# First batch of a fused attention and feed-forward kernel in units of 128, 256 and 384 tokens, with keys ahead of queries and weights in column quarters

## Chip, cores, metric

One NeuronCore of one Trainium2 chip. The metric is the device time of one execution in microseconds (us). TensorE is PE in the profile, VectorE is DVE, ScalarE is ACT, GpSimd is POOL, SyncE is SP.

## The reference

Routed attention (4 batches, 8 heads, 768 tokens of 64), then a SwiGLU feed-forward block with RMS norm (3072 x 512, inner size 1536):

```python
q_assign = argmax(q_n . c_n); k_assign = argmax(k_n . c_n)      # 16 clusters per head
scores = where(q_assign == k_assign, scale * q @ k.T, -1e9)     # per batch and head
attn = softmax(scores) @ v                                       # [4, 8, 768, 64]
x = attn.transpose(0, 2, 1, 3).reshape(3072, 512)
xn = x / sqrt(mean(x * x, -1) + 1e-6) * rms_g
out = (silu(xn @ w_gate) * (xn @ w_val)) @ w_out                 # [3072, 512], fp32
```

## The kernel before

It works in *units* of 384 tokens, two per batch. A unit is attention over 8 heads (three steps of two 384-column score matmuls and one exponential of 768 columns each), then the feed-forward part. Attention waits on ACT, so the feed-forward work of the unit before is given out between the score steps as filler. The order is fixed by the program, and each engine takes its instructions in that order. The accumulators of a head pair have **one** PSUM buffer, which DVE must empty before the next pair can start:

```python
ps_s = pool("ps_s", 2, space=PSUM); ps_a = pool("ps_a", 1, space=PSUM); ps_g = pool("ps_g", 3, space=PSUM)

def pv(u, h):                              # attention times values of one head
    if h % 2 == 0:
        accs[u] = ps_a.tile([P, 2, HT, D + 1], F32, tag="acc", name="acc")
    ...                                    # 18 matmuls into acc
    if h % 2:
        nc.vector.reciprocal(inv, acc[:, :, :, D])
        nc.vector.tensor_tensor(dst, acc[:, :, :, :D], ...)     # the eviction, into x
```

DVE makes the keys of a coming group of four heads (`kcast`: eight casts). For group 2 they are part of `second`, the preparation that fills unit 1 and precedes the transposes of the normed tokens:

```python
def second(h=h, n=n):                      # in group_work(g)
    trans(g, h, 1)
    qcast(g, h)
    kcast(g, h)                            # DVE
    vcast(n); load_qk(n + NQ); load_v(n + NV)

# the list that fills unit 1
prep = group_work(2) + group_work(3)
fill += [rms(0)] + prep[:8] + ffn[:12] + [output_weights] + spread(ffn[12:], prep[8:])   # shortened; ffn = xtrans x4, gv x16
```

In unit 0, which has no feed-forward work to fill it, ten filler matmuls (`busy(1, False)`) are emitted between the score steps.

The softmax here doesn't subtract the row's maximum and nothing guards it: scores larger than these inputs give would overflow.

Of the kernel before, what the change touches and what calls it, by code (L numbers as in the profile page):

```python
# [22 lines left out]
def kernel(  # L23
# [23 lines left out]
    NU = 2 * B  # L47
# [4 lines left out]
    WARM = 5  # L52
# [25 lines left out]
    def load_qk(n, kq=None):  # L78
        if n >= B * H:
            return  # L80
        staged[n] = stage.tile([P, 2, ST, D], F32, tag="qk", name="qk")
        nc.sync.dma_start(out=staged[n][:, 0], in_=src(q, n))
        (kq or nc.sync).dma_start(out=staged[n][:, 1], in_=src(k, n))
# [9 lines left out]
    for n in range(HG):  # L93
        load_qk(n, nc.scalar)
    for n in range(HG, NQ):
        load_qk(n)
# [17 lines left out]
    def rsqrt(ms, n):  # L114
        half = small.tile([P, n], I32, tag=f"half{n}", name="half")
        nc.vector.tensor_scalar(half, ms.bitcast(I32), 1, None, op0=ALU.logical_shift_right)
        yi = small.tile([P, n], I32, tag=f"yi{n}", name="yi")
        nc.vector.tensor_scalar(yi, half, -1.0, float(0x5F3759DF), op0=ALU.mult, op1=ALU.add)
        y = yi.bitcast(F32)
        for i in range(3):  # L120
            a = small.tile([P, n], F32, tag=f"na{n}", name="na")
            nc.vector.scalar_tensor_tensor(a, y, -0.5, y, op0=ALU.mult, op1=ALU.mult)
            a2 = small.tile([P, n], F32, tag=f"nb{n}", name="nb")
            nc.vector.tensor_mul(a2, a, ms)
            y2 = small.tile([P, n], F32, tag=f"ny{n}", name="ny")
            nc.vector.scalar_tensor_tensor(y2, a2, 1.5, y, op0=ALU.add, op1=ALU.mult)
            y = y2
        return y
# [51 lines left out]
    def load_gv(c):  # L180
        nc.gpsimd.dma_start(out=wg[:, c], in_=moe_w_gate[c * P:(c + 1) * P])
        nc.gpsimd.dma_start(out=wv[:, c], in_=moe_w_val[c * P:(c + 1) * P])
# [7 lines left out]
    def trans(g, h, part):  # L190
        if (h % 2, part) == (0, 0):
            qkT[g, h // 2] = qk32.tile([P, 2, 2, UQ], F32, tag="qkT", name="qkT")
# [7 lines left out]
    def qcast(g, h):  # L200
        for e in range(2):
            nc.gpsimd.tensor_copy(qext[g % 4][:D, h, e * UQ:(e + 1) * UQ], qkT[g, h // 2][e * D:(e + 1) * D, h % 2, 0])  # L202

    def kcast(g, h, early=False):
        for e in range(2):
            to, of = kext[g % 4][:D, h, e * UQ:(e + 1) * UQ], qkT[g, h // 2][e * D:(e + 1) * D, h % 2, 1]
            if early:
                nc.scalar.activation(to, of, ACT.Copy, scale=1.0 / ZS)
            else:
                nc.vector.tensor_scalar_mul(to, of, 1.0 / ZS)  # L210
# [11 lines left out]
    def cluster_steps(g, m, h0=0, h1=HG, early=False):  # L222
# [17 lines left out]
        def back():  # L240
            oh = asg.tile([P, UQ], BF16, tag="oh", name="oh", bufs=4)
            nc.vector.transpose(oh[r], of["ohT"][r])  # L242
            put.append((g, (kext if m else qext)[g % 4], oh, h0, h1))
# [13 lines left out]
    put = []  # L257

    def place(qq, kq):

        (g, *_, h0, h1) = put[0]
        for h in range(h0, h1):
            for (_, ext, oh, _, _), on in zip(put, (qq, kq)):
                for e in range(2):
                    on.dma_start(out=ext[D:D + NC, h, e * UQ:(e + 1) * UQ],  # L265
                                 in_=oh[32 * h + e * NC:32 * h + (e + 1) * NC])
        put.clear()
# [4 lines left out]
    def scores(u, h, i):  # L272
        b, hf = divmod(u, 2)
        g, hh = b * 2 + h // HG, h % HG
        if i == 0:
            pT[u, h] = ptp.tile([P, ST, UQ], BF16, tag="pT", name="pT")
        ps = ps_s.tile([P, 2, 512], F32, tag="s", name="s")
        for j in range(2):
            kc = 2 * i + j
            nc.tensor.matmul(ps[:, j, :UQ], lhsT=kext[g % 4][:KR, hh, kc * P:(kc + 1) * P],  # L280
                             rhs=qext[g % 4][:KR, hh, hf * UQ:(hf + 1) * UQ], start=True, stop=True)
        nc.scalar.activation(pT[u, h][:, 2 * i:2 * i + 2], ps[:, :, :UQ], ACT.Exp, bias=off, scale=scale * ZS)  # L282
# [3 lines left out]
    def pv(u, h):  # L286
        b = u // 2
# [6 lines left out]
        for t in range(HT):  # L294
# [3 lines left out]
        if h % 2:  # L298
            inv = small.tile([P, 2, HT], F32, tag="inv", name="inv")
            invs[u] = inv  # L300
            nc.vector.reciprocal(inv, acc[:, :, :, D])  # L301
            dst = xs[u][:, :, (h - 1) * D:(h + 1) * D].rearrange("p t (h d) -> p h t d", d=D)
            nc.vector.tensor_tensor(dst, acc[:, :, :, :D], inv.unsqueeze(3).broadcast_to([P, 2, HT, D]), op=ALU.mult)
# [13 lines left out]
    def rms(u):  # L317
        x = xs[u]
        for t in range(HT):
            squares(u, t, True)  # L320
        ss = small.tile([P, HT], F32, tag="sm", name="sm")
        nc.vector.tensor_add(ss, sq[u][:, 0], sq[u][:, 1])
        ms = small.tile([P, HT], F32, tag="ms", name="ms")
        nc.vector.tensor_scalar(ms, ss, 1.0 / DM, 1e-6, op0=ALU.mult, op1=ALU.add)
        y = rsqrt(ms, HT)
        for t in range(HT):
# [4 lines left out]
    def xtrans(u, c):  # L331
# [3 lines left out]
        for t in range(HT):  # L335
            nc.tensor.transpose(ps[:, t * P:(t + 1) * P], xn[u][:, t, c * P:(c + 1) * P], ident)
        nc.vector.tensor_scalar_mul(xnT[u][:, c], ps, gcol[:, c:c + 1])
# [3 lines left out]
    def gv(u, f, val):  # L341
# [3 lines left out]
        ps = ps_g.tile([P, UQ], F32, tag="gen", name="val" if val else "gate")  # L345
        for c in range(CC):
            nc.tensor.matmul(ps, lhsT=w[:, c, f * P:(f + 1) * P], rhs=xnT[u][:, c], start=c == 0, stop=c == CC - 1)  # L347
        last = u == NU - 1
        if not val:
            th = gate.tile([P, UQ], F32, tag="th", name="th")  # L350
            if last:
                nc.scalar.activation(th, ps, ACT.Silu)
                gates[u] = th
            else:
                nc.scalar.activation(th, ps, ACT.Tanh, scale=0.5)  # L355
                nc.vector.scalar_tensor_tensor(th, th, 1.0, ps, op0=ALU.add, op1=ALU.mult)  # L356
                gates[u] = th
        elif last:
            nc.vector.tensor_mul(gvT[u][:, f], gates[u], ps)
        else:  # L360
            nc.vector.scalar_tensor_tensor(gvT[u][:, f], gates[u], 0.5, ps, op0=ALU.mult, op1=ALU.mult)  # L361
# [3 lines left out]
    def out_mm(u, t, part):  # L365
        b, hf = divmod(u, 2)
# [4 lines left out]
        if part == 2:  # L371
# [3 lines left out]
            nc.sync.dma_start(out=rows[:, 2 * t + hf], in_=o)  # L375


    def group_work(g):
# [15 lines left out]
        w.append((0.0, lambda: place(nc.gpsimd, nc.gpsimd)))  # L394
# [14 lines left out]
    def ffn_work(u):  # L409
        w = [(0.18, lambda c=c: xtrans(u, c)) for c in range(CC)]  # L410
        for f in range(FC):
            w.append((0.64, lambda f=f: gv(u, f, False)))
            w.append((0.64, lambda f=f: gv(u, f, True)))
        return w

    def out_work(u):
        return [(0.86, lambda t=t, p=p: out_mm(u, t, p)) for t in range(HT) for p in range(3)]


    def t0(h):  # L420
        for part in range(2):
            trans(0, h, part)
        qcast(0, h)
        if NQ + h < H:
            load_qk(NQ + h)
# [3 lines left out]

    trans(0, 0, 0)  # L430
    centroids_t()
    trans(0, 0, 1)
    load_qk(NQ)
    trans(0, 1, 0)
    qcast(0, 0)
    qcast(0, 1)
    clusters0(0, 0)
    trans(0, 1, 1)
    load_qk(NQ + 1)
    for n in range(HG):  # L440
        load_v(n)
    clusters0(0, 1)
    for h in range(2, HG):
        for part in range(2):
            trans(0, h, part)
        qcast(0, h)
    place(nc.gpsimd, nc.sync)
    for n in range(HG, H):
        load_v(n)
    nc.sync.dma_start(out=gcol, in_=moe_rms_g.rearrange("(c p) -> p c", p=P), allow_slow_non_contiguous=True)  # L450
    kcast(0, 0, True)
    kcast(0, 1, True)
    vcast(0)
    vcast(1)
    for m in range(2):
        clusters0(2, m)
    for h in range(HG):
        for part in range(2):
            trans(1, h, part)
        qcast(1, h)  # L460
        if h == 1:
            place(nc.gpsimd, nc.sync)
            vcast(2)
            vcast(3)
    busy(2)

    def second_group():
        kcast(0, 2, True)
        kcast(0, 3, True)
        for m in range(2):  # L470
            scores_c(1, m)
        for c in range(CC):
            load_gv(c)
        for n in range(HG, H):
            vcast(n)
        place(nc.sync, nc.sync)
        for h in range(HG):
            kcast(1, h)

    def output_weights():  # L480
# [86 lines left out]
```

## Time and profile before

| | before |
|---|---|
| time | 375.94 us, median of 3 (375.48 to 376.34) |
| span of the profiled run, mean granted clock | 371.8 us, 0.982 |
| output weights, issue to landing (median) | 13.5 us |
| key and query cluster rows ("placements", 12 KB), 10 to 32 us | 2.3 to 5.2 us median by queue |

The prediction below shows the busy shares, the clock and the stretches of this profile.

(Timeline: start, length, engine, line, operation, count, idle time before it. Names: `s` scores, `pT` exponentials, `acc` attention times values, `x` a unit's attention output, `xn` the normed tokens, `tx` and `xnT` the same transposed, `tq` transposed queries or keys, `qext` and `kext` queries and keys with their cluster rows, `th` a gate after tanh, `gvT` gate times val, `o` outputs, `wo` the output weights.) I call what lies between them **the stage**: attention of the last 384 tokens of the first batch, 42.8 us long here. The changed kernel has exactly the same stage as its unit 2.

### The profile page before, as it was taken

The numbers are of one execution on the slowest core, as the hardware profiler recorded it, in microseconds if no ns is written. First come the engines' busy times: TensorE is split into PE (matmuls) and PEld (weight loads), VectorE is DVE, ScalarE is ACT, GpSimd is POOL, SyncE is SP. The second block draws the span as 40 slices with busy tenths as digits, with TensorE's granted clock in tenths as the row PEclk, the third lists the DMA queues.
The fourth block names the chain that finished last, engine by engine and source line by source line (L and its number), as shares of the span: only waits on it lengthen the run. The fifth ranks groups of instructions, "written<-read, shape, count | busy, mean of one in ns | idle before, by whom it ended". The sixth has DMA issues, their size and how long they took to land.

```text
span 371.8 us, 8016 instructions
## 1 busy us (share of the span) xinstructions
PE 351.1 (94%) x3026; PEld 210.5 (57%) x3026; DVE 241.7 (65%) x573; ACT 260.0 (70%) x461; POOL 107.6 (29%) x221
## 2 busy tenths in 40 slices
PE   7979867999999999999999999999999999999995
PEld 3535544565566555655566555655566656664552
DVE  4981186678756966777756966777656565667432
ACT  4797983798669775888668775888767876762320
POOL 3694071089615170325315170325300000000000
PEclk9976998999999999999999999999999999999999
DMA  8649999726126101450022001000020002001002
GB/s 273 188 95 210 249 329 248 159 63 180 58 85 198 63 20 56 129 155 14 13 85 86 4 20 57 30 0 13 12 86 2 3 0 86 2 1 58 28 3 85
DMA packets 24967, 32.03 MB, mean 86 GB/s; under 512 B 4960, under 2 KB 20832, under 8 KB 24928
## 3 DMA queue, kind: packets, MB, share of 16 engines
q1 hardware_dynamic: 18288, 24.72, 20.5%
q0 software_dynamic: 6064, 6.00, 8.6%
q10 hardware_dynamic: 576, 0.79, 0.6%
q8 instruction: 24, 0.39, 0.4%
q14 instruction: 15, 0.12, 0.1%
HBM read 28.35 MB, written 6.29 MB: 93 GB/s over the span
## 4 chain that ended last, share of the span: by engine, by line
PE 71%; ACT 12%; DVE 11%; issue 3%; DMA 1%; DVEq 0%; SPq 0%; ACTq 0%
PE o L370 17%; PE gate L347 13%; PE val L347 13%; PE s L280 13%; PE acc L296 7%; ACT pT L282 7%; PE tq L196 3%; PE sc L251 3%; DVE th L356 2%; ACT th L355 2%; DVE kext L210 2%; ACT qkT L198 1%; ACT xn L315 1%; DVE oh L242 1%; DVE o_sb L373 1%
## 5 line engine op out<-in xcount | busy, mean ns | idle before, releaser
L282 ACT ACTIVATE pT<-s,off 128x768 bf16<-128x768 f32 x192 | 170.9, 902 | 48.3 <-PE s L280 47.3
L280 PE MATMUL s<-qext,kext 80*128 80x384 bf16 x384 | 96.6, 335 | 5.6 <-ACT pT L282 5.2
L347 PE MATMUL val<-xnT,wv 128*128 128x384 bf16 x384 | 78.7, 327 | 0.9 <-DVE th L356 0.6
L347 PE MATMUL gate<-xnT,wg 128*128 128x384 bf16 x384 | 78.9, 327 | 0.1
L370 PE MATMUL o<-wo,gvT 128*128 128x512 bf16 x288 | 70.3, 379 | 0.5
L356 DVE SCALAR_TENSOR_TENSOR th<-th,gate 128x384 f32<-128x384 f32 x84 | 46.4, 553 | 30.3 <-ACT th L355 29.2
L280 PEld LDWEIGHTS <-kext 80*128 80x128 bf16 x384 | 37.2, 100 | 45.2 <-issue 18.5
L202 POOL CAST qext<-qkT 64x384 bf16<-64x384 f32 x64 | 33.7, 526 | 97.2 <-ACT qkT L198 95.3
L355 ACT ACTIVATE th<-gate 128x384 f32<-128x384 f32 x84 | 41.2, 490 | 25.9 <-PE gate L347 22.0
L361 DVE SCALAR_TENSOR_TENSOR gvT<-th,val 128x384 bf16<-128x384 f32 x84 | 46.3, 552 | 9.1 <-PE val L347 2.6
L296 PEld LDWEIGHTS <-pT 128*128 128x128 bf16 x1152 | 44.9, 99 | 9.7 <-issue 0.8
L347 PEld LDWEIGHTS <-wv 128*128 128x128 bf16 x384 | 36.5, 98 | 23.7 <-issue 3.2
L347 PEld LDWEIGHTS <-wg 128*128 128x128 bf16 x384 | 36.6, 98 | 22.7 <-issue 0.7
L296 PE MATMUL acc<-vbf,pT 128*128 128x65 bf16 x1152 | 47.0, 195 | 0.5 <-ACT pT L282 0.5
L370 PEld LDWEIGHTS <-gvT 128*128 128x128 bf16 x288 | 26.7, 97 | 26.2 <-issue 1.0
L265 POOL DMA_DIRECT2D qext<-oh x56 | 27.2, 491 | 39.5 <-DVE oh L242 38.5
L196 PE MATMUL tq<-ident_f,qk 128*128 128x128 f32 x192 | 32.6, 289 | 3.1 <-DMA qk<-in_q_dram 1.2
L198 ACT COPY qkT<-tq 128x384 f32<-128x384 f32 x64 | 29.1, 484 | 5.8 <-PE tq L196 5.6
L210 DVE TENSOR_SCALAR kext<-qkT 64x384 bf16<-64x384 f32 x56 | 24.6, 440 | 12.0 <-ACT qkT L198 11.2
L196 PEld LDWEIGHTS tq<-ident_f,qk 128*128 128x128 f32 x192 | 22.8, 145 | 12.8 <-ACT qkT L198 3.2
L265 POOL DMA_DIRECT2D kext<-oh x48 | 23.3, 489 | 16.6 <-DVE inv L301 15.0
L373 DVE COPY o_sb<-o 128x512 f32<-128x512 f32 x24 | 16.4, 689 | 12.9 <-PE o L370 12.7
(60 smaller groups left out, 232.0 us busy)
## 6 DMA issues: line engine op xcount, KB each, us to landing
qk<-in_q_dram SPq DMA_DIRECT2D x32, 192.0 KB, 3.9
vs<-in_v_dram SPq DMA_DIRECT2D x32, 192.0 KB, 3.8
out_dram<-o_sb SPq DMA_DIRECT2D x24, 256.0 KB, 2.0
qk<-in_k_dram SPq DMA_DIRECT2D x28, 192.0 KB, 3.8
wg<-in_moe_w_gate_dram POOLq DMA_DIRECT2D x4, 384.0 KB, 9.1
wv<-in_moe_w_val_dram POOLq DMA_DIRECT2D x4, 384.0 KB, 10.3
wo<-in_moe_w_out_dram POOLq DMA_DIRECT2D x3, 512.0 KB, 13.5
qext<-oh POOLq DMA_DIRECT2D x56, 12.0 KB, 1.6
```

The source lines that it names most:

```text
L196: nc.tensor.transpose(ps[:, i * P:(i + 1) * P], qk[:, part, 2 * i:2 * i + 2].rearrange("p t d -> p (t d)"), ident_f)
L198: nc.scalar.copy(qkT[g, h // 2][:, h % 2, part], ps)
L202: nc.gpsimd.tensor_copy(qext[g % 4][:D, h, e * UQ:(e + 1) * UQ], qkT[g, h // 2][e * D:(e + 1) * D, h % 2, 0])
L265: on.dma_start(out=ext[D:D + NC, h, e * UQ:(e + 1) * UQ], in_=oh[32 * h + e * NC:32 * h + (e + 1) * NC])
L280: nc.tensor.matmul(ps[:, j, :UQ], lhsT=kext[g % 4][:KR, hh, kc * P:(kc + 1) * P], rhs=qext[g % 4][:KR, hh, hf * UQ:(hf + 1) * UQ], start=T ...
L282: nc.scalar.activation(pT[u, h][:, 2 * i:2 * i + 2], ps[:, :, :UQ], ACT.Exp, bias=off, scale=scale * ZS)
L296: nc.tensor.matmul(acc[:, h % 2, t], lhsT=pT[u, h][:, kc, t * P:(t + 1) * P], rhs=vbf[g % 4][:, hh, kc % HT * 2 + kc // HT], start=kc == 0 ...
L347: nc.tensor.matmul(ps, lhsT=w[:, c, f * P:(f + 1) * P], rhs=xnT[u][:, c], start=c == 0, stop=c == CC - 1)
L355: nc.scalar.activation(th, ps, ACT.Tanh, scale=0.5)
L356: nc.vector.scalar_tensor_tensor(th, th, 1.0, ps, op0=ALU.add, op1=ALU.mult)
L361: nc.vector.scalar_tensor_tensor(gvT[u][:, f], gates[u], 0.5, ps, op0=ALU.mult, op1=ALU.mult)
L370: nc.tensor.matmul(outs[u], lhsT=gvT[u][:, f, t * P:(t + 1) * P], rhs=wo[:, f], start=f == 0, stop=f == FC - 1)
```

## The change

Intent: reach feed-forward work earlier. The first 128 tokens are a unit of their own, so their norm can run after 18 instead of all 24 of the first exponentials; the next 256 are interleaved with them by heads; keys are prepared and placed ahead of queries, so that the first scores start earlier; gate and value weights arrive in column quarters, so that the first quarter suffices for the first gates. The diff, cut to its core:

```diff
-    NU = 2 * B
+    UNITS = [(0, 0, 1), (0, 1, 2), (0, 3, 3)] + [(b, c, HT) for b in range(1, B) for c in (0, HT)]   # batch, first tile, tiles
+    NU = len(UNITS)
-    WARM = 5
+    WARM = 8
-    def load_gv(c):
-        nc.gpsimd.dma_start(out=wg[:, c], in_=moe_w_gate[c * P:(c + 1) * P])
-        nc.gpsimd.dma_start(out=wv[:, c], in_=moe_w_val[c * P:(c + 1) * P])
+    def load_gv(i):
+        c = slice(i * DF // 4, (i + 1) * DF // 4)
+        for w, of in ((wg, moe_w_gate), (wv, moe_w_val)):
+            nc.gpsimd.dma_start(out=w[:, :, c], in_=of[:, c].rearrange("(c p) f -> p c f", p=P))
@@ start: heads 2 and 3 of group 0 get their keys from GpSimd, half of the query columns is placed first
+    for h in (2, 3):
+        kcast(0, h, nc.gpsimd)
+    vcast(2)
+    vcast(3)
+    load_gv(0)
+    def second_clusters():
+        scores_c(1, 0)
+        place(nc.gpsimd, 1, 0, 0, (0,))
+        for h in range(HG):
+            kcast(1, h)
+        ...                                  # value casts, three weight quarters, other query halves, output weights
@@ the order of units
-    for u in range(NU): ...                  # one unit after the other; filler matmuls in unit 0
+    f0 = ffn_work(0)
+    attention([(0, 0), (0, 1), (1, 0), (1, 1), (0, 2), (0, 3), (1, 2), (1, 3), (0, 4), (0, 5), (0, 6), (0, 7)], [],
+              hooks={(0, 1, 0): second_q, (1, 0, 1): second_clusters, (0, 7, 0): second_batch})
+    attention([(1, h) for h in range(4, H)], f0[:CC + 8], 5, {(1, 4, 1): lambda: rms(0)})
+    for u in range(2, NU):
+        ...                                  # as before, with the leftovers, norm and outputs of units of any size
```

The output weights are now issued in the first attention stretch, before any gate, and no filler matmul is left in it.

## The prediction

> **What bounds the kernel now.** I read the page's busy shares and slices first, then the busy time by stretch, then the timelines of PE, ACT, DVE and GpSimd up to 100 us, and last the DMA issues.
>
> ```profile
> PE 351.1 (94%) x3026; PEld 210.5 (57%) x3026; DVE 241.7 (65%) x573; ACT 260.0 (70%) x461; POOL 107.6 (29%) x221
> ...
> PEclk9976998999999999999999999999999999999999
> DMA  8649999726126101450022001000020002001002
> ```
>
> TensorE is the bound over the whole, so any time at which it does no useful work at the start is paid in full at the end. The clock and DMA rows show that only the first sixth is different: the clock dips there, and the DMA engines are full there and nowhere else.
>
> ```profile
> 20.00:30.00 10.00, 7.10 (x61) 3.98 (x54) 8.53 (x18) 8.62 (x13) 9.78 (x20) 0.70 0.50 92
> 30.00:40.00 10.00, 9.73 (x100) 5.69 (x99) 0.77 (x3) 8.52 (x11) 1.85 (x4) 0.79 1.10 215
> 40.00:50.00 10.00, 7.29 (x72) 4.66 (x71) 3.42 (x13) 9.92 (x25) 1.68 (x4) 1.00 0.97 269
> 50.00:60.00 10.00, 5.14 (x49) 3.26 (x48) 8.70 (x20) 4.29 (x9) 7.05 (x12) 0.91 1.04 314
> 60.00:70.00 10.00, 10.00 (x90) 5.75 (x88) 5.61 (x11) 7.87 (x12) 0.00 (x0) 0.92 1.15 251
> ...
> 100.00:200.00 100.00, 99.03 (x915) 61.76 (x914) 70.42 (x166) 74.89 (x130) 30.96 (x64) 1.00 0.27 84
> ```
>
> (Columns: PE, PEld, DVE, ACT, POOL busy; granted clock; DMA share; GB/s.) From 100 us PE is busy 99% at full clock. Before 60 us it is not, and part of its busy time is filler (17 `warm` matmuls, 7.2 us). ACT is the pacemaker there: 8.5 to 9.9 of 10.
>
> ```profile
> 18.30 0.81 PE L280 MATMUL s<-qext,kext 80*128 80x384 bf16 x4
> 33.92 8.31 ACT L282 ACTIVATE pT<-s,off 128x768 bf16<-128x768 f32 x10 [0.23 <-PE s L280]
> 53.47 4.10 DVE L210 TENSOR_SCALAR kext<-qkT 64x384 bf16<-64x384 f32 x8
> 58.08 0.44 PE L336 MATMUL tx<-ident,xn 128*128 128x128 bf16 x3 [3.58 <-DVE xnT L337]
> 58.40 1.44 PE L347 MATMUL gate<-xnT,wg 128*128 128x384 bf16 x4
> 62.44 0.81 PE L347 MATMUL gate<-xnT,wg 128*128 128x384 bf16 x4
> ```
>
> The first scores run at 18.3 us; then all 24 exponentials of the first 384 tokens (0.83 us each in a row) must pass before their RMS norm, and the first feed-forward matmul comes only at 58.4. The wait of 3.58 us just before it is the norm behind eight key casts on DVE.
>
> How much is lost: I take spacing from the starts of neighbouring timeline rows. Gate, val and scores of 384 columns: 0.65 us for 4, so 0.163 each; the 65-column products 0.54 for 18, so 0.030; output 0.86 for 4, so 0.216; fp32 transposes 0.36 for 3, so 0.12; one cluster product of a group 0.78; a small transpose about 0.06. Times the counts of the whole kernel: 384 x 0.163 + 768 x 0.163 + 288 x 0.216 + 1152 x 0.030 + 192 x 0.12 + 16 x 0.78 + 96 x 0.06 = 326 us of useful work in a span of 372. By 58.4 us the groups show 60 scores, 72 transposes, 162 products, 32 cluster rows (4 x 0.78) and 12 small transposes: 27 us of work. So **31 of the 46 lost us lie before the first gate**. That is what the change is after.
>
> **What the Trainium skill says.**
> - "TensorE: Matmul & The Clock Gate", Part 1: a window of about 3.4 us of idleness halves the clock, a busy one restores it. The trace agrees in kind: 0.70 and 0.79 in 20 to 40 us. The same page, under the issue gap, gives N / 2.4 + 2.5 ns for a warm matmul: 162.5 ns at 384 columns, as measured (0.163). For 128 it gives 55.8, so splitting 384 into 128 + 256 costs about 2.5 ns per extra matmul, provided the weight loads keep hidden; the products at 0.030 us each, each with its own 128-column load, say that they do.
> - "GPSIMD Engine Reference", section 2.1: the first call of a freshly loaded kernel library costs about 6 us with no visible instruction. The kernel before shows no such gap (its GpSimd runs copies and DMA issues only). In the built order of the changed one a custom instruction stands just before the first tensor-scalar on GpSimd, which is new (key casts of heads 2 and 3). I take it for such a load.
> - "DMA: Bandwidth & Descriptors", queues and arbitration: engines alternate between queues that have work. The trace fits: weights issued at 25 to 29 us landed in 9 to 10 us median beside other loads.
>
> **The change, part by part.**
> 1. *Units of 128, 256, 384.* The number of exponentials per head stays 3 (768 columns each), so ACT has the same 24, but the norm of the first 128 tokens needs only the 8 of unit 0 and what is interleaved before it: 18 of 24 up to head 4 of unit 1. Added: 96 more gate/val matmuls (96 x 2.5 ns = 0.2 us), 12 more tanh (ACT +1 us), 24 more DVE steps and one more rsqrt chain (13 x 0.2; DVE +4 to 6 us). DVE is at 65%, so off the path, but the new norm chain (0.3 + 13 x 0.2 + 0.6 + 4 x 0.25, about 5 us) lies just before the first gate.
> 2. *Keys ahead, half the query columns placed first.* The first one-hot (keys) is ready about 10.5 us, the queries 13.3. Eight warm matmuls instead of five put the first transposes at about 4.9 instead of 4.3. GpSimd then casts (4 x 0.53, to 11.1), issues 4 key rows (13.2) and 2 query rows (14.3); landing 2 us later gives first scores at about 16.8. Worth **1.5 us**.
> 3. *GpSimd's queue.* From 14.3: 2 value casts (15.3), 2 query casts (16.4), library (22.4), 4 key casts at 0.53 (24.5), 2 value casts (25.5), 2 weight issues at 0.8, as wo's (27.1), 4 query casts (29.2), 4 placements (31.2). Scores of head 2 want the first key cast at 23.6 (16.8 + 6 exponentials and 4 copies, 6 x 0.81 + 4 x 0.40): nearly met. Heads 4 to 7 want their placements at 28.9 (6 more exponentials): they land at 31.7 to 33.2. **ACT loses about 3.5 us** there in all, and PE goes cold.
> 4. *First gate.* 4 exponentials (to 35.2), 2 of unit 1 (36.9), products and norm chain 5.5 us: first gate near **42.5**, against 58.4. The last two exponentials of unit 1 stand behind it in PE's order, so unit 2 starts about 44.5 (the matching stage of before started at 45.2: small, because the waits of 3 and the norm eat what 2 and the interleaving gain).
> 5. *Unit 2.* PE: 48 scores 7.8, products 4.3, rest of the 128-token gates 3.6, 16 of 24 gate/val of 256 tokens 7.0, transposes 5.8, clusters 3.1, output 2.6, small 0.5: 34.7 us; ACT 33. Before, the same stretch from 60 to 91.4 us held 30.2 us of work (96%). So 36 us, plus waits. It ends at 80.5 plus waits, against 91.4: before, this stage began with 13 us of starving (45 to 58.4), which the 128-token work now fills.
> 6. *Weights in quarters.* The first quarter (0.79 MB) is issued at 26 us, long before 42.5. The other three (2.36 MB), issued about 32.5 to 38, share the engines with the second batch (4.7 MB, from 34.5 on) and the output weights (1.57 MB, issued about 43). By 60 us before had moved some 13.5 MB at 0.25 to 0.31 MB per us when loaded. With equal shares the gates' quarters are down by 51, the output weights at about 61. The first output matmuls now come near 57 instead of 95.5: **a new wait of 2 to 4 us** on them.
>
> ```profile
> wo<-in_moe_w_out_dram POOLq DMA_DIRECT2D x3, 512.0 KB, 13.5
> ```
>
> Sum: unit 2 ends at 80.5 + 3 = 83.5 or so, 7.9 earlier than 91.4. At that point less is left: before, 8 gate/val of 384 (5.2) and 36 outputs (7.8), 13.0 us; after, 8 of 256 (3.5) and 24 outputs (5.2), 8.7: 4.3 us less. Rest of the kernel unchanged and PE-bound. 7.9 + 4.3 = 12.2 us; I take off 1.3 for cold clock and in-order waits that I can't place: **375.9 - 10.9 = 365.0 us**.
>
> **Rivals.**
> - *GpSimd becomes the bound of the start.* If the load takes 10 us or more beside busy DMA engines, or its tensor-scalar runs at twice a cast's 0.53 us, placements, value casts and weight issues slide by 4 to 7 us: 368 to 371. For it: everything the first heads need passes that one queue. Against: it had 6.5 us of idleness in 0 to 30 us before.
> - *DMA bound.* Work that starts 15 us earlier wants 8.6 MB earlier; if the quarters' short rows (1.5 KB read, 0.75 KB written) lower the rate to 0.2 MB per us, gates and group-2 transposes wait too: 368 to 370. For it: shares over 1.0 from 30 to 70 us. Against: 20 to 30 us stood half idle.
> - *All of it is hidden.* No load gap, DMA keeps up: unit 2 starts at 41 and ends at 77 to 78: 360 to 361.
> - *Half clock.* With the filler gone from units 0 and 1, PE is about 65% busy and may run at half clock until the first gate: its 10 us there become 20 of 18 to 40, near ACT's pace: 1 to 3 us, partly counted.
>
> **Range and chances.** The spread of the terms (load 0 to 10 us but half hidden, weights wait 0 to 6, cold clock 0 to 3) gives 360.5 to 370.5. The border of 2% is 368.4; two of the rivals must strike together to pass it. Faster by over 2%: 0.79; within 2%: 0.20; slower: 0.01.
>
> **What would show it.** First scores near 17 us; a gap of 5 us or more on GpSimd before the first key cast with tensor-scalar; ACT idle before heads 4 to 7 with GpSimd or its DMA as releaser; first gate near 42.5; PE at 95% or more from then but for a wait on wo near 57; half clock somewhere in 18 to 40; after 100 us the same picture as before, shifted. Wrong would be: first gate after 50 us (the norm or GpSimd took all), gates waiting on weights for more than 4 us, or spacings of 128-column matmuls well over 0.06 us, which would make the split itself cost.

## More of the kernel before

In the timeline (start, length, engine, line, operation, count, idle time before it) I count score matmuls: 48 per unit.

```profile
43.57 0.48 PE L280 MATMUL s<-qext,kext 80*128 80x384 bf16 x2 [0.51 <-ACT pT L282]
...
45.19 0.71 PE L296 MATMUL acc<-vbf,pT 128*128 128x65 bf16 x18
...
86.41 0.49 PE L280 MATMUL s<-qext,kext 80*128 80x384 bf16 x2
...
87.52 0.71 PE L296 MATMUL acc<-vbf,pT 128*128 128x65 bf16 x18
```

By 43 us the counts show 48 scores, by 86 us 96. So the pair at 43.57 opens unit 1 and the pair at 86.41 opens unit 2; in both cases the products of the last head of the unit before follow (45.19 and 87.52), as the program orders.

## The result

The changed kernel takes 380.47 us, median of 4 runs (379.89 to 381.11); before took 375.71 (373.59 to 376.34) in the same rounds. The ratio is 1.0137 with a 95% interval of 1.0092 to 1.0183: **1.4% slower, within the band called the same, and 15 us from the prediction**. (Ratios are the mean time of one kernel's runs over the mean of the other's runs of the same rounds, so not quite the ratio of the medians quoted.) The profiled runs are 371.8 and 379.2 us long, 7.4 apart; before's profiled run was its fastest (373.53), so the pair of profiles shows some 2.6 us more than the medians do.

The page of the changed kernel: busy shares, then the clock in 40 slices of the span.

```profile
PE 357.5 (94%) x3173; PEld 224.9 (59%) x3173; DVE 247.9 (65%) x622; ACT 259.1 (68%) x469; POOL 114.6 (30%) x227
...
PEclk9985589899999999999999999999999999999999
```

The clock has a deeper hole than before (two slices at 5). The stretches (PE, PEld, DVE, ACT, POOL busy; granted clock; DMA share; GB/s):

```profile
30.00:40.00 10.00, 8.36 (x84) 6.82 (x84) 2.71 (x10) 6.03 (x7) 9.95 (x18) 0.51 0.81 120
40.00:50.00 10.00, 9.27 (x77) 7.10 (x77) 5.02 (x24) 7.33 (x14) 1.42 (x2) 0.50 1.28 236
50.00:60.00 10.00, 8.97 (x130) 7.22 (x129) 5.70 (x21) 8.29 (x21) 0.00 (x0) 0.96 1.16 267
60.00:70.00 10.00, 7.08 (x70) 5.04 (x68) 8.87 (x26) 7.56 (x18) 6.30 (x12) 1.00 1.04 338
70.00:80.00 10.00, 8.76 (x76) 5.05 (x76) 5.26 (x14) 4.32 (x7) 0.00 (x0) 0.83 0.29 103
```

From 30 to 50 us PE runs at half clock for the whole time (30.2 to 50.7 us in windows of 1 us, after 20.0 to 23.4; before had 24.0 to 34.3), and ACT, the pacemaker of before (8.52 and 9.92 busy), falls to 6.03 and 7.33: its exponentials now wait for scores. Later, 60 to 80 us has holes again, and after that PE is nearly full (97.99 of 100 us between 100 and 200). The timeline of PE shows what they are:

```profile
18.48 0.83 PE L284 MATMUL s<-qext,kext 80*128 80x128 bf16 x12 [0.95 <-DMA qext<-oh]
...
31.37 0.49 PE L302 MATMUL acc<-vbf,pT 128*128 128x65 bf16 x6 [3.38 <-DVE x L309]
...
47.68 0.71 PE L357 MATMUL gate<-xnT,wg 128*128 128x128 bf16 x4
...
52.34 0.81 PE L284 MATMUL s<-qext,kext 80*128 80x384 bf16 x4
...
71.24 0.37 PE L344 MATMUL tx<-ident,xn 128*128 128x128 bf16 x2 [3.19 <-DVE xnT L345]
...
97.09 0.81 PE L284 MATMUL s<-qext,kext 80*128 80x384 bf16 x4
```

Two waits of over 3 us, both on DVE. DVE's own timeline shows that it was not late with the awaited work itself, but had something else ahead of it:

```profile
27.35 3.33 DVE L214 TENSOR_SCALAR kext<-qkT 64x384 bf16<-64x384 f32 x8
30.60 0.17 DVE L307 RECIPROCAL inv<-acc 128x4 f32<-128x4 f32 x1
30.80 0.42 DVE L309 TENSOR_TENSOR x<-acc,inv 128x256 f32<-128x256 f32 x1
...
66.38 3.85 DVE L214 TENSOR_SCALAR kext<-qkT 64x384 bf16<-64x384 f32 x8
70.15 0.18 DVE L307 RECIPROCAL inv<-acc 128x6 f32<-128x6 f32 x1
...
70.84 0.60 DVE L345 TENSOR_SCALAR xnT<-tx,gcol 128x256 bf16<-128x256 bf16 x2
```

At 27 us the eight key casts of group 1 stand ahead of the eviction of the first head pair of unit 1, and the accumulator has only one buffer. At 66 us the eight key casts of group 2 stand ahead of the first evictions of normed, transposed tokens; before had the same at 53.47 (shown in the prediction), once.

**Where the time went, by the stage.** The stage runs from 43.57 to 86.41 us in before, and from 52.34 to 97.09 us in the changed kernel. It starts 8.8 us later and ends 10.7 us later, at which point 4.3 us less work is left over (that sum of the prediction stands: 8.7 against 13.0 us). 10.7 - 4.3 = 6.4 of the 7.4 us between the two profiles. The split, meant to start this stage as early as before and shorten it, made it start late.

### The profile page after: what moved, and what is told of

Same layout as the page of the kernel before. It is cut to its first block, busy times and chain, and to the rows that moved or that the text cites. A ratio compares the mean times of both kernels' runs of the same rounds, so it can differ in the third digit from the quotient of the medians. Undisturbed runs are those within 1.5% of the kernel's fastest.

```text
span 379.2 us, 8425 instructions
## 1 busy us (share of the span) xinstructions
PE 357.5 (94%) x3173; PEld 224.9 (59%) x3173; DVE 247.9 (65%) x622; ACT 259.1 (68%) x469; POOL 114.6 (30%) x227
## 3 DMA queue, kind: packets, MB, share of 16 engines
q0 software_dynamic: 9200, 6.03, 9.7%
## 4 chain that ended last, share of the span: by engine, by line
PE 73%; DVE 10%; ACT 7%; POOL 4%; issue 3%; DMA 2%; SPq 0%; DVEq 0%; ACTq 0%
PE gate L357 16%; PE val L357 15%; PE s L284 13%; PE o L379 12%; PE acc L302 8%; PE tq L200 5%; ACT pT L288 4%; PE sc L255 3%; DVE o_sb L382 2%; DVE xn L334 1%; ACT xn L322 1%; DMA qext<-oh 1%; DMA qk<-in_k_dram 1%; ACT th L365 1%; PE warm L112 1%
## 5 line engine op out<-in xcount | busy, mean ns | idle before, releaser
L284 PE MATMUL s<-qext,kext 80*128 80x384 bf16 (+2 forms) x432 | 98.6, 325 | 1.9 <-DMA qext<-oh 0.9
L357 PE MATMUL val<-xnT,wv 128*128 128x384 bf16 (+2 forms) x432 | 80.7, 310 | 1.8 <-DVE th L366 1.5
L357 PE MATMUL gate<-xnT,wg 128*128 128x384 bf16 (+2 forms) x432 | 81.1, 310 | 0.3 <-DVE gvT L370 0.2
L366 DVE SCALAR_TENSOR_TENSOR th<-th,gate 128x384 f32<-128x384 f32 (+2 forms) x96 | 48.3, 503 | 35.4 <-ACT th L365 34.1
L206 POOL CAST qext<-qkT 64x384 bf16<-64x384 f32 x64 | 32.6, 519 | 109.2 <-ACT qkT L202 107.5
L284 PEld LDWEIGHTS <-kext 80*128 80x128 bf16 x432 | 42.2, 105 | 34.1 <-issue 10.3
L357 PEld LDWEIGHTS <-wv 128*128 128x128 bf16 x432 | 40.1, 98 | 25.8 <-issue 5.9
L302 PEld LDWEIGHTS <-pT 128*128 128x128 bf16 x1152 | 46.7, 100 | 14.3 <-issue 3.5
L370 DVE SCALAR_TENSOR_TENSOR gvT<-th,val 128x384 bf16<-128x384 f32 (+2 forms) x96 | 48.0, 500 | 10.0 <-PE val L357 2.4
L302 PE MATMUL acc<-vbf,pT 128*128 128x65 bf16 x1152 | 49.7, 197 | 5.0 <-DVE x L309 3.4
L365 ACT ACTIVATE th<-gate 128x384 f32<-128x384 f32 (+2 forms) x96 | 43.0, 450 | 15.5 <-PE gate L357 15.2
L357 PEld LDWEIGHTS <-wg 128*128 128x128 bf16 x432 | 40.0, 98 | 21.5 <-issue 1.2
```

What stands on the lines that cost most here:

```text
L206: nc.gpsimd.tensor_copy(qext[g % 4][:D, h, e * UQ:(e + 1) * UQ], qkT[g, h // 2][e * D:(e + 1) * D, h % 2, 0])
L284: nc.tensor.matmul(ps[:, j, :w] if nt == HT else flat[:, j * w:(j + 1) * w], lhsT=kext[g % 4][:KR, hh, kc * P:(kc + 1) * P], rhs=qext[g % ...
L302: nc.tensor.matmul(acc[:, h % 2, t], lhsT=pT[u, h][:, kc, t * P:(t + 1) * P], rhs=vbf[g % 4][:, hh, kc % HT * 2 + kc // HT], start=kc == 0 ...
L357: nc.tensor.matmul(ps, lhsT=w[:, c, f * P:(f + 1) * P], rhs=xnT[u][:, c, :n], start=c == 0, stop=c == CC - 1)
L365: nc.scalar.activation(th, ps, ACT.Tanh, scale=0.5)
L366: nc.vector.scalar_tensor_tensor(th, th, 1.0, ps, op0=ALU.add, op1=ALU.mult)
```

## Experiments

Four theories of why: the start is too **sparse** for full clock once the filler is gone (A, where the texts use letters); **the key casts of group 1** stall the accumulators and so start the cold stretch (B); **the key casts of group 2** before the norm cost what they did in before, again (C); **value loads** crowd the placements at the start, so first scores gain nothing (D). The rival to all: the split itself, or the quarters, cost more than they bring. The kernels are the changed one with the edit shown, unless said otherwise. Before's medians were 375.55 (e1 to e4), 373.89 (e5, e6, n1, n2), 374.78 (e8, e9, n3, n4) and 374.38 us (e4_again, p1 to p3); each ratio is to those.

| run | median us | ratio to before, 95% interval | stage starts, ends |
|---|---|---|---|
| before | 375.71 | 1 | 43.6, 86.4 |
| changed | 380.47 | 1.0137 (1.0092 to 1.0183) | 52.3, 97.1 |
| e1_fill | 378.69 | 1.0102 (1.0065 to 1.0138) | 50.1, 94.8 |
| e2_keys_late | 378.29 | 1.0093 (1.0056 to 1.0130) | 51.2, 95.9 |
| e3_prep_late | 377.46 | 1.0057 (1.0018 to 1.0097) | 52.8, 93.8 |
| e4_keys_prep_late | 373.88 | 0.9972 (0.9924 to 1.0019) | 47.1, 88.7 |
| e5_all | 374.84 | 1.0026 (0.9982 to 1.0069) | 46.7, 91.3 |
| n1_before_keys_late (from before) | 369.06 | 0.9872 (0.9829 to 0.9916) | 43.8, 82.7 |
| n2_no_split | 377.80 | 1.0084 (1.0030 to 1.0137) | 44.4, 90.6 |
| e6_v_late | 380.63 | 1.0175 (1.0133 to 1.0217) | 51.4, 96.2 |
| e8_qk_first | 373.91 | 1.0007 (0.9944 to 1.0070) | 49.8, 92.7 |
| e9_rows | 374.49 | 1.0007 (0.9952 to 1.0062) | 49.8, 90.8 |
| n3_no_split_mended | 369.95 | 0.9890 (0.9834 to 0.9945) | 43.6, 82.6 |
| n4_before_qk_first (from before) | 368.82 | 0.9862 (0.9795 to 0.9928) | 42.7, 81.5 |
| e4_again | 374.33 | 0.9983 (0.9951 to 1.0015) | 49.4, 90.2 |
| p1_rms_ahead | 382.84 | 1.0204 (1.0167 to 1.0240) | 49.5, 94.8 |
| p2_pairs | 374.25 | 0.9986 (0.9957 to 1.0015) | 49.0, 90.9 |
| p3_both | 382.76 | 1.0214 (1.0180 to 1.0248) | 49.7, 96.0 |

The stage times come from one profile each, by the same count of scores, to about 0.1 us; e4 and its repeat differ by 2.3 us at the start, so only larger differences are read from them. The intervals of e1 and e2 overlap that of the changed kernel: a gain of some 2 us in one run is at the edge of what these ratios can tell. No run is faster or slower by 2% beyond doubt (e6, n4, p1 and p3 are unclear at that mark).

**e1_fill: filler back in the start (theory A).**

```diff
+            if at < warm:
+                busy(1, False)               # one 512-column filler matmul at each of 21 score steps of units 0 and 1
```

> The changed kernel with one filler matmul of 512 columns behind each score step of units 0 and 1 up to the first gate (21 in all). Theory A (the clock stays at half from 31 to 51 us because the matmuls of units 0 and 1 are too sparse without filler): the clock is back at 1.00 by about 36 us, the first gate comes near 44.5 instead of 47.7, unit 2's first scores near 49 instead of 52.3, time about 377. Theory B (the wait of 3.4 us on DVE at 27.5 us is what matters, density is not): clock and time as in the changed kernel, 380. Rival C (the split itself costs, through many small ACT and DVE steps): 380, or more, since filler only adds work.

Measured 378.69 us. The stretches and the timeline of PE of this run:

```profile
30.00:40.00 10.00, 9.16 (x104) 6.67 (x105) 1.53 (x6) 7.48 (x10) 9.84 (x16) 0.75 0.94 144
40.00:50.00 10.00, 7.75 (x101) 5.89 (x100) 5.80 (x28) 8.16 (x18) 0.00 (x0) 1.00 1.26 243
```

```profile
29.85 0.49 PE L302 MATMUL acc<-vbf,pT 128*128 128x65 bf16 x6 [3.17 <-DVE x L309]
...
68.93 0.27 PE L344 MATMUL tx<-ident,xn 128*128 128x128 bf16 x2 [3.19 <-DVE xnT L345]
```

Sparse work is why the clock stays low (0.75 and 1.00 instead of 0.51 and 0.50; half clock from 28.2 to 35.0 us), but both DVE waits are as before, and the stage starts only 2.2 us earlier. A is right about the clock and wrong as the whole cause.

**e2_keys_late: group 1's key casts behind the eviction (theory B).**

```diff
         place(nc.gpsimd, 1, 0, 0, (0,))
-        for h in range(HG):
-            kcast(1, h)
-              hooks={..., (1, 0, 1): second_clusters, (0, 7, 0): second_batch})
+              hooks={..., (1, 0, 1): second_clusters, (0, 2, 0): second_keys, (0, 7, 0): second_batch})   # second_keys = the four kcasts
```

> The changed kernel with the key casts of heads 4 to 7 moved on DVE behind the eviction of unit 1's first head pair; no filler. Both A and B: the wait of TensorE on the eviction at 27.5 us (3.4 us) goes. B: without it the clock does not fall, unit 2 starts near 46.5, time 374 to 375. A: it falls to half all the same somewhat later because the work stays sparse, unit 2 starts near 50, time 378. C: no more than the 3.4 us at best, and given back.

Measured 378.29 us. Timeline of PE and one stretch:

```profile
34.35 0.84 PE L302 MATMUL acc<-vbf,pT 128*128 128x65 bf16 x12 [0.95 <-DVE x L309]
...
70.01 0.32 PE L344 MATMUL tx<-ident,xn 128*128 128x128 bf16 x2 [3.19 <-DVE xnT L345]
```

```profile
30.00:40.00 10.00, 7.89 (x91) 6.42 (x92) 5.24 (x14) 7.17 (x9) 9.95 (x17) 0.63 0.58 87
```

The wait of 3.38 us is down to 0.95, yet the clock falls all the same, at 32.6 us and ahead of that wait, after 6.6 us (from 26) in which PE was busy 72% of the time with no wait over 0.5 us. So no long stall is needed to make it cold; B fails as the cause of the clock. (This run's first scores also came later, at 19.24, with half clock from 18.9 to 25.7. The casts now stand ahead of the next pair's eviction, so part of the wait only moved: 2.01 us in e4_again.)

**e3_prep_late: group 2's key casts behind the norm's evictions (theory C).**

```diff
                 qcast(g, h)
-                kcast(g, h)
+                if g != 2:
+                    kcast(g, h)
-        fill += ... + o[-1:] + spread(ffn[CC:CUT], prep[n:])
+        fill += ... + o[-1:] + ([(0.0, lambda h=h: kcast(2, h)) for h in range(HG)] if u == 2 else []) + spread(ffn[CC:CUT], prep[n:])
```

> The changed kernel with group 2's eight key casts moved on DVE behind the four evictions of unit 1's norm transposes; nothing else. If the wait of 3.2 us at 68 us and the half clock after it are what made the changed kernel lose 5 us between 65 and 75 us: about 375.5. If output weights that land late are the true bound there (theory D, as the prediction had it): the output matmuls wait instead and no more than 2 us are won, 378.5.

Measured 377.46 us, between the two expectations and 3.0 us below the changed kernel by medians, though its wait at 31 us happened to be longer (5.14 us). The norm's wait of 3.19 us is gone (0.19 is left) and the stage is 41.0 instead of 44.8 us long. C holds, with the size of the wait.

**e4_keys_prep_late and e5_all: e2 and e3 together, then e1 as well.**

> Both moves of key casts together, no filler. If the two waits are independent the savings of the two runs add up: 371 to 373.5, faster than before (375.7). If what is won early is given back at a later wait: no better than the better of the two.

> The changed kernel with both moves of key casts and the filler in units 0 and 1. The run with both moves still ran at half clock from 29 to 43 us, for 13 of its first 60 us. If filler keeps the clock up there (theory A): the first gate at 40 to 41 instead of 43.0, time 371 to 372.5. If ACT's order and the norm set the pace by then and the clock does not matter any more: 373.5 to 374.5, as without filler.

e4 measured 373.88 us and 374.33 when repeated: level with before, and short of the 371 to 373.5 expected. Both moves together bring 6.1 to 6.6 us by medians, 5.8 to 6.2 by ratios; 2.2 + 3.0 lies within the noise of that, so the savings add up, and more is not shown. e5, with the clock held up as well (1.00 from 20 to 40 us), brings nothing on top: 374.84. Its timeline of PE shows why:

```profile
66.53 1.74 PE L379 MATMUL o<-wo,gvT 128*128 128x512 bf16 x4 [2.74 <-DMA wo<-in_moe_w_out_dram]
```

That is the wait on the output weights that the prediction expected. It was hidden in the changed kernel only because everything else was later: the weights had landed by about 65 us (issued at 39.2 to 41.4, 23.5 us at most), and the first output matmul came at 66.69. In e4 0.5 us of it shows.

**n1_before_keys_late: the kernel before, with only the key casts of group 2 moved.**

```diff
                 qcast(g, h)
-                kcast(g, h)
+                if g != 2:
+                    kcast(g, h)
-            fill += ... prep[:8]] + ffn[:12] + ...
+            fill += ... prep[:8]] + ffn[:4] + [(0.0, lambda h=h: kcast(2, h)) for h in range(HG)] + ffn[4:12] + ...
```

> Control: the kernel before with the same move of group 2's key casts behind the norm transposes of unit 0, nothing of the change. It had 3.58 us of wait there and half clock for some 3 us after. If the move is worth what it was in the changed kernel (3 us): 372 to 373. Then the move and not the change is what makes the mended kernel fast. If the transposes' own copies or DMA hold it: 375.

Measured 369.06 us, 1.3% faster than before and better than the 372 to 373 expected. The half clock that followed the wait in before (58.1 to 61.6 us) is gone with it. Of the 3.58 us wait before the first gate 0.17 is left, and the first gate, at 58.40 in before, starts at 55.13 in this run's timeline of PE:

```profile
55.13 0.99 PE L347 MATMUL gate<-xnT,wg 128*128 128x384 bf16 x4
```

So a mend that has nothing to do with the split gains more than the split with all its mends.

**n2_no_split and n3_no_split_mended: the change without the split.** n2 keeps keys ahead, quarters and early weights, but has units of 384 and the filler again. n3 adds both moves of key casts and issues the output weights after the first gates, as before does.

```diff
-    UNITS = [(0, 0, 1), (0, 1, 2), (0, 3, 3)] + [(b, c, HT) for b in range(1, B) for c in (0, HT)]
+    UNITS = [(b, c, HT) for b in range(B) for c in (0, HT)]
@@ n3 only, in second_clusters
-        for c in range(0, FC, 4):
-            load_o(c)
```

> The changed kernel without its split: units of 384 tokens all through, in before's order from unit 1 on and with before's filler, but keys ahead, weights in quarters, and the new start. If the split is what costs (C, fewer output matmuls to cover the norms, two norm chains, sparse matmuls): near or below before, 373 to 376. If the new start or the quarters cost: 378 to 381.

> The changed kernel without its split, with both moves of key casts and the output weights issued late again, as before does. Against the kernel before with only the norm's key casts moved (369), this tells what the new start and the column quarters are worth by themselves. If the start is worth the 1.5 us that I predicted: 367.5 to 368.5. If early weights still delay group 2's queries and keys: 370 to 373.

n2 measured 377.80 us, just under the upper of the two expectations. Besides the key casts (a wait of 3.02 us on DVE x), PE waits for the second batch, in whose way the early weights now are (0.74 and 0.18 us more beside these two):

```profile
48.52 0.55 PE L200 MATMUL tq<-ident_f,qk 128*128 128x128 f32 x3 [1.85 <-DMA qk<-in_q_dram]
...
52.31 0.90 PE L200 MATMUL tq<-ident_f,qk 128*128 128x128 f32 x3 [0.95 <-DMA qk<-in_q_dram]
```

n3 measured 369.95 us. Sent in one call with e8 and e9, the split in its mended form, it is 0.9890 against their 1.0007, with intervals that at most touch (0.9945 is the upper end of n3's, 0.9944 and 0.9952 the lower ends of theirs). **The split costs about 1.2%, some 4 us**, and since n3 is no faster than n1, keys ahead and quarters bring nothing that these runs can see. Two reservations: n3 also has the filler, which brings the split nothing (e5), and issues the output weights later, which was not tried with the split. And keys ahead did not do their work in n3: its first scores came at 18.14 us against 18.43 in n1, and at 31 us it waited 2.16 us for a placement. What an earlier start would be worth is not shown.

**e6_v_late, e8_qk_first, e9_rows, n4_before_qk_first: loads.** e6 loads values 4 to 7 and the norm's weights behind the placements. e8 (on e4) and n4 (on n1) load the second batch's queries and keys ahead of its values. e9 (on e4) loads the weights in row quarters, as before.

```diff
@@ e6_v_late
-    for n in range(3, H):
-        load_v(n)
+    load_v(3)                                # 4 to 7 and gcol only behind the placements
@@ e8_qk_first, n4_before_qk_first, in second_batch
+        for n in range(H, H + NQ):
+            load_qk(n)
         for n in range(H, H + NV):
-            if n < H + NQ:
-                load_qk(n)
             load_v(n)
@@ e9_rows
-            nc.gpsimd.dma_start(out=w[:, :, c], in_=of[:, c].rearrange("(c p) f -> p c f", p=P))
+            nc.gpsimd.dma_start(out=w[:, i], in_=of[i * P:(i + 1) * P])
```

> The changed kernel with the value loads of heads 4 to 7 and the norm weights issued behind the placements of heads 2 and 3. In the changed kernel the first query placement took some 5 us to land beside those loads and the first scores came at 18.5 us instead of the 16.8 that I had predicted. If the loads slow it: landing 2 to 3 us, first scores at 16.5 to 17, and about 1.5 us of time at most, 379, as the key casts then hold TensorE at the same place. If not: unchanged.

> The changed kernel with both moves of key casts, and with the second batch's queries and keys loaded ahead of all its values. In the run with both moves and the filler, the output matmuls waited 2.7 us for the output weights at 66 us, with the DMA engines full from 34 to 70 us. Theory D (with the waits on DVE mended, DMA is the bound of this stage): fewer bytes ahead of the output weights, their landing 3 to 5 us earlier, no wait on them, and time 371 to 372.5. If the stage is paced by ACT and the norm instead: 373 to 374.5, as without the reordering.

> The changed kernel with both moves of key casts, but gate and value weights again loaded in row quarters, at the same places of the program. The first gate needs all four row quarters. If the column quarters are what lets the 128-token unit start its feed-forward: the first gate waits on the weights until about 48 instead of 43, and the time is 376 to 378. If not: 373 to 374.5.

> The kernel before with group 2's key casts behind the norm transposes and with the second batch's queries and keys loaded ahead of its values. It waited 2.5 us in four pieces for those queries and keys at 47 to 52 us. If DMA is the bound there: the waits go and 366.5 to 368 result, the best of all. If ACT's copies are just behind: 369, as without.

In e6 the first scores start at 17.08 us instead of 18.48, as D has it, but the whole gain goes into the next wait, on DVE x, which grows from 3.38 to 5.33 us: 380.63 us, nothing won. D is right about the placements, and in this kernel, with that wait next, worth nothing. e8 and e9 stay where e4 is: e8 still waits 1.75 us for the output weights, so fewer bytes ahead did not do what was expected, and e9's first gate comes at 44.4 us without a wait on weights (e4: 43.0 and 44.5), so column quarters are not what lets it start. n4 takes the waits for the second batch out of n1 (0.85 and 0.95 us, among others, 2.5 in all), of which 1.5 come back as a longer wait of a val on `th` (1.91 instead of 0.46 us), and measures 368.82 us: the best version, 1.4% faster than before, though not told apart from n1 (0.9862 against 0.9872).

**p1_rms_ahead, p2_pairs, p3_both, e4_again: what e4 still lacks.** p1 (on e4) emits the norms of units 1 and 2 ahead of the last leftover gate groups of the unit before them, so that these cover the norm; p2 (on e4) orders gate, gate, val, val in the two small units; p3 has both and e8's load order.

```diff
@@ p1_rms_ahead: left = leftover gate and val groups of unit u - 2; at = 6 (u = 2) or 4 (u = 3) before its end
-        fill = left + [rms(u - 1)] + prep[:n]
+        fill = left[:at] + [rms(u - 1)] + left[at:] + prep[:n]
@@ p2_pairs: groups of f and f + 1
-        gate f, val f, gate f + 1, val f + 1
+        gate f, gate f + 1, val f, val f + 1
```

> The mended changed kernel once more, as the base for the other three of this call: 373.9 us again, ratio to before 0.995 to 1.001. In its trace the PE waits over 0.15 us between 60 and 112 us add up to 4.0 us (the before with the same mend: 1.3 us).

> The mended changed kernel with the norms of units 1 and 2 started ahead of the last 6 and 4 leftover gate/val groups of the unit before, so that these cover the norm. Theory 'too little work covers the second and third norm': its waits on DVE xn (0.8 us) and part of the idleness near 100 us go, 1 to 2 us won, 372.2 us. Rival 'the small gate steps themselves pace the stretch' (tanh and two DVE steps per 128 or 256 columns): nothing won, because the norm's 13 DVE steps then lengthen the waits on th and gvT: 373.5 to 374.5.

> The mended changed kernel with units 0 and 1 in the order gate, gate, val, val instead of gate, val, gate, val, so that a val has one more matmul group ahead of it to cover tanh and its DVE step. Theory 'small gate steps pace it': waits of val on th (0.6 us and more before 60 us) go, 0.5 to 1.5 us won, 372.7 us. Rival 'too little cover for norms': nothing, 373.9. Against a gain: three PSUM buffers, two of them then held by gates, so gates may wait on gvT instead.

> Both of these and the second batch's queries and keys loaded ahead of its values. If both covers are what the split lost, 371 us or less, close to the undivided mended kernel (370); if neither, 373.5 to 374.5, and the loss sits in the added fixed work of a smaller unit (one more norm chain, 24 more DVE steps and 12 more tanh) or in the output weights.

p2 changes nothing (374.25). p1 is 8.5 us slower than e4_again, against all of my expectations (the rival had named the mechanism, the norm's steps ahead of `th`, and put it at nothing). Its timelines of PE and of DVE:

```profile
60.09 0.58 PE L357 MATMUL val<-xnT,wv 128*128 128x128 bf16 x4 [3.05 <-DVE th L366]
...
104.27 1.01 PE L357 MATMUL val<-xnT,wv 128*128 128x256 bf16 x4 [3.18 <-DVE th L366]
```

```profile
102.61 1.28 DVE L334 TENSOR_SCALAR xn<-x,ny 128x512 bf16<-128x512 f32 x3
103.80 0.41 DVE L366 SCALAR_TENSOR_TENSOR th<-th,gate 128x256 f32<-128x256 f32 x1
```

The gate steps on DVE now stand behind the norm's chain (100.04 to 103.80 us), val waits for them, and each of the two waits of 3.1 us is followed by cold clock (0.71 and 0.66 in 60 to 70 and 100 to 110 us). It is the same fault as the two in the changed kernel, made anew elsewhere: **3 to 5 us for every chain of 3 us or more that stands on DVE ahead of a step PE waits for** (3.0 us for the wait of 3.19 that e3 takes out, 4.8 for that of 3.58 in n1, 4.3 for each of the two here). p3 repeats it (382.76).

## Why the prediction was wrong

Predicted 10.9 us faster, measured 4.8 us slower. The steps that failed are 4 and 5, start and length of the stage: the sum had no term for what stands ahead of PE's evictions in DVE's queue (waits of 3.38 and 3.19 us), counted half clock as 1 to 3 us at most, and took its difference from a wrong landmark. By its own steps:

1. *Units of 128, 256 and 384* (step 1): the split costs PE nothing, as said: four gate matmuls of 128 columns are 0.22 to 0.23 us apart (0.056 each). DVE's added work is at the upper end of what was said (6.2 us for 4 to 6). What it left out is that a small unit has little PE time to cover its fixed steps: see below; that this costs time was not isolated.
2. *Keys ahead* (step 2): failed. First scores at 18.48, not 16.8: the first placements took 4.5 us to land beside the value loads, not the 2 assumed. In this kernel it would have been worth nothing anyhow, by e6.
3. *GpSimd's queue* (step 3): failed in its cause. No library gap (below); the four casts took 4.91 us, more than twice a plain cast's time each, as the rival "GpSimd becomes the bound" had allowed for, so the queue was about 3 us less long than I had put down. The 3.5 us I gave it did come, as 3.38 us, but by luck: they came from **DVE's order**. No library gap and weights in time were also the premises of the rival "all of it is hidden" (360 to 361); both held, and it was the furthest off. No rival named DVE's order: I never asked what stands ahead of the eviction in DVE's queue, though the order of instructions was there to read.
4. *First gate and start of the stage* (step 4): 47.68 instead of 42.5, and 52.34 instead of 44.5. The rival "half clock" was given 1 to 3 us and "partly counted"; half clock lasted from 30.2 to 50.7 us, after 3.4 us of it at 20, together 23.9 us against 10.2 in before ahead of the stage. Runs: e4 starts the stage 3 to 5 us earlier with the casts moved, e1 2.2 us earlier with the clock held; with everything mended (e5) it still starts at 46.7. Before starts it at 43.6 with no norm ahead of it. The norm of the first unit stands in PE's order ahead of the last two heads' scores, as step 4 itself says, and stops ACT meanwhile (e5's timeline, below).
5. *The stage* (step 5): 44.8 us long instead of 36 + 3. The term "plus waits 3" failed: the wait on the norm behind eight key casts, 3.19 us, which **I had seen and quoted in the profile of before** and did not carry over to the same place in the changed kernel; e3 takes it out and the stage shrinks by 3.8 us.
6. *The reference point* (step 5): "ends at 91.4" in before was misread. 91.4 is a later pair of scores of unit 2; the first is at 86.41. The start, "45.2", is the products after the first scores at 43.57. With the right end, the prediction's own terms give 86.4 - 83.5 = 2.9 instead of 7.9, that is about 370 us. Nearly 5 of the 15 us are this.

Check of the sum: 13.6 us of the stage's end (97.1 against 83.5) are 7.8 (late start) plus 5.8 (longer stage). 375.9 + (97.1 - 86.4) - 4.3 = 382.3, against 380.5 measured; the rest is within the 2.6 us by which the two profiles differ more than the medians.

What was right: 4.3 us less work left at the stage's end, the wait on the output weights (0.5 us in e4, 1.75 in e8, 2.74 in e5, where the rest is mended), no gates waiting on weights, the same picture from 110 us on. The DMA rival is half shown: n2 has 3.7 us of such waits for the second batch; in the changed kernel those transposes come later, and none is seen.

**Why the split loses even when mended.** Compare e4 with n1: the stage starts at 47.1 to 49.4 against 43.8, is 40.9 to 41.6 us long against 38.9, and ends 6.0 to 7.6 us later with 4.3 us less left: 1.7 to 3.3 of the 2.8 to 4.4 us between their spans (370.7 and 372.3 against 367.9). So the larger part is the late start. Cold clock is some of it: e4 had 13.7 us of half clock ahead of the stage and its repeat, the same program, 20.5, and the repeat started 2.3 us later. But e5 had only 3.4 us and still starts 3 us after before, which had 10.2. Its timeline of ACT shows the norm's part:

```profile
37.87 3.28 ACT L288 ACTIVATE pT<-s,off 128x768 bf16<-128x768 f32 x4
42.65 0.28 ACT L365 ACTIVATE th<-gate 128x128 f32<-128x128 f32 x1 [1.50 <-PE gate L357]
43.50 0.90 ACT L288 ACTIVATE pT<-s,off 128x768 bf16<-128x768 f32 x1 [0.57 <-PE s L284]
...
45.36 0.90 ACT L288 ACTIVATE pT<-s,off 128x768 bf16<-128x768 f32 x1
...
47.24 1.69 ACT L288 ACTIVATE pT<-s,off 128x768 bf16<-128x768 f32 x2 [0.31 <-PE s L284]
```

From 41.2 to 47.2 us ACT runs two exponentials and sits idle for 2.4 us, waiting for a gate and for scores; before that it ran one every 0.82 us. The scores of the last heads come behind norm, transposes and gates. This is read from the trace; no run moved the norm out of the way. The changed kernel's gate steps show a second reason (groups by form: busy us, mean ns of one):

```profile
L366 DVE SCALAR_TENSOR_TENSOR th<-th,gate 128x384 f32<-128x384 f32 x72 | 39.9, 554 | 28.0 <-ACT th L365 26.8
...
L366 DVE SCALAR_TENSOR_TENSOR th<-th,gate 128x128 f32<-128x128 f32 x12 | 3.4, 285 | 4.5 <-ACT th L365 4.5
```

A third of the columns still takes half the time (285 against 554 ns). A gate with its val has two such steps: 0.57 us on DVE against 0.45 us on PE at 128 columns, 1.11 against 1.30 at 384. In small units DVE is the slower of the two, and PE has more waits of 0.2 to 1 us on it (th, gvT): 3.6 us in all in e4 up to 115 us, against 1.0 in n1 and 1.6 in n3. That this is a cause was not isolated: p2, the one run that went at it, moved nothing. **Open**: the 1 us or so after the stage, and how much of the late start of e4 each of norm order, cold clock and the rest of the moved key casts is worth.

## What to carry to other kernels

Before splitting work to start a consumer earlier, list for each engine what stands ahead of the step that will become critical; here two groups of eight casts, each ahead of one eviction, cost some 6 us together, and moving one of them in the *old* kernel was worth 1.3% by itself. Treat a wait of 3 us on PE as 3 to 5: in these runs the clock fell with each, and thin work was slow to bring it back (half clock until 50.7 us in the changed kernel, until 35.0 with filler). And check the landmarks that a difference is taken from by counting instructions: one misread end made 5 us of the predicted gain.

## What the Trainium skill lacked or had wrong

- "TensorE: Matmul & The Clock Gate", Part 1: the table has an idle window of about 3.4 us halve the clock. Its window fits: in all 18 profiles every stretch of half clock at the start is a whole multiple of 3.41 us (3.4, 6.8, 10.2, 13.7, 17.1, 20.5 or 23.9). "Idle" does not: in e2_keys_late the clock fell at 32.6 us after 6.6 us in which PE was busy 72% with no wait over 0.5 us, in before at 24.0 us after a wait of 2.2 us. Nor does one busy window always restore it: in the changed kernel PE was shown busy 100% from 33.7 to 37.1 us, and half clock lasted until 50.7. The page's passage on a second failure mode names short gaps as a cause, but no passage puts a figure on how dense work must be. In windows of 3.41 us counted from a run's first fall, to about 105 us, PE was shown busy 2 to 69% in those just before a fall (though some at 49% kept full clock) and 93% or more in those just before a return.
- "GPSIMD Engine Reference", section 2.1: about 6 us with no visible instruction for the first call of a freshly loaded kernel. The page does not say which instructions pay this. The tensor-scalar's first call on GpSimd, with two `MODIFY_POOL_CONFIG` at 16.5 and 16.6 us just ahead of it, shows no gap:

```profile
15.62 0.95 POOL L206 CAST qext<-qkT 64x384 bf16<-64x384 f32 x2
16.64 4.91 POOL L214 TENSOR_SCALAR kext<-qkT 64x384 bf16<-64x384 f32 x4
```

- No page gives a figure for a GpSimd tensor-scalar; "GPSIMD Engine Reference", section 4.1, calls one-input elementwise work roughly line-rate. Here one took 1.17 us for 64 x 384, fp32 to bf16 (mean of 4), against 0.52 us for a plain cast of the same size on GpSimd (mean of 64) and 0.45 us for the tensor-scalar on DVE (mean of 56).
- "DMA: Bandwidth & Descriptors", arbitration: turns between queues with work are stated, not what a small transfer pays beside large ones. Here a placement of 12 KB landed in 4.5 us (median of the first four, beside value loads) against 1.6 us for those of GpSimd's queue over the whole kernel.
